# First entry: two low parts of w_spatial on GpSimd, a quarter of w_in later, value and gate by chunks

## The chip, the cores and the metric

The kernel runs on one core of one Trainium2 chip. The metric is the device time of one execution in microseconds (us). Five engines work side by side, each through a queue of its own in order: TensorE (PE, matmuls into PSUM; its weight loads are listed as PEld), VectorE (DVE), ScalarE (ACT), GpSimd (POOL) and SyncE (SP, which issues most DMAs).

## What is computed

For each of 8 batch entries (`b`), with 8 heads, 576 positions, head size 64, 32 packed queries, `d_model` 512 and `d_ff` 1024:

```python
p_packed = sm_attn(p, k, v)              # softmax attention of 32 packed queries
x = sm_attn(q, p_packed, p_packed)       # every position attends to the 32
h = relu(x @ w_in); u, v = h[..., :512], h[..., 512:]
v_n = (v - mean(v)) / sqrt(var(v) + 1e-6)        # over the 512
v_s = einsum('ts,bsd->btd', w_spatial, v_n) + b_spatial[None, :, None]
out = (u * v_s) @ w_out
```

`w_in` and `w_out` come in as 64-bit floats.

## The kernel before, in words

**Precision.** Matmuls of the feed-forward part use fp32r operands. A value is split in a high part (a cast to fp32r, `_h`) and a low part (the value less its high part, `_l`), and a product is made of the terms high-high, high-low and low-high.

**The value** (`FeedForward.value`, line 532) makes the right half of `h` in chunks of 128 positions: group `g` has the chunks 2g and 2g+1 (`js`), and group 2 is the tail of 64 positions with its two parts to be added. In entry 0 the three terms (`ns`) run one behind the other: a_h with m_h, a_h with m_l, a_l with m_h. Behind it come, chunk by chunk: `relu` (ACT, out of PSUM), `stats` (DVE, two operations), `inverse` (POOL, two operations on one column: add eps, power -1/2), `norm` (DVE), `norm_hi` (ACT cast into v_h) and `norm_lo` (v_l; on DVE, for some chunks of entry 0 on POOL). For the tail, `relu(2)` copies one part out on ACT and `relu_tail` adds it to the other, in PSUM, on DVE.

**The gate** (`FeedForward.gate`, line 647) multiplies the chunks of the normalised value by w_spatial. `es` are the four blocks of 128 of the 512 features, `cs` the chunks, and `parts` the terms: "h" and "m" take v_h with the high and the low part of w_spatial, "l" takes v_l with the high part, "t" is the tail and the bias. Each block has a PSUM quarter (`on(0)` to `on(3)`, tiles ps0 to ps3), and its result is copied out by `gate_keep` on ACT in entry 0.

**w_spatial** (line 184 on) lies in SBUF as four chunks and a tail (number 4). `spatial_hi(c)` casts its high part on ACT. The low part is made on PE in `spatial_rest(c)` (line 210): identity times the chunk, plus minus-identity times the high part, into PSUM; `spatial_lo(c)` (line 219) then copies it to `wsp_l` on ACT. `rest(lo, x, hi, eng)` (line 82) is a subtraction on a given engine.

**w_in** is loaded in four quarters, and each is turned from 64-bit to fp32 by `to_f32` (line 147), a generator with five steps, one for each `next`: an ACT conversion of the low word; two DVE operations on the high word (a shift with mask, and a combination); two POOL adds; an ACT `Abs`; and a last DVE operation that writes `w_in_sb`. `conv_u0` and `conv_u1` are the two quarters of the left half, which first serve `att.mix(0)` (line 1091). w_out is turned in the same way (`out01`, `out23`).

**Order.** PE, DVE, ACT and POOL execute in the order in which the program calls them (`InOrder`, line 35). Entry 0 is written out by hand (lines 892 to 1198), together with the first attention steps of the next entries; entries 1 to 7 run in a loop (line 1204) that the change doesn't touch. Behind the changed lines of entry 0 stand `nxt.pack_scores(by_turns(2, 3))` (line 1067), which writes ps2 and then ps3, and the rest of the gate for blocks 3 and 2.

Of the kernel before, what the change touches and what calls it, by code (L numbers as in the profile page):

```python
# [49 lines left out]
def body(ctx: ExitStack, tc, q, k, v, vt, p, w_in, w_sp, b_sp, w_out, out):  # L50
# [11 lines left out]
    pe, dve, act, pool = (  # L62
        InOrder(tc, e) if x in PIN else e
        for e, x in ((nc.tensor, "t"), (nc.vector, "v"), (nc.scalar, "s"), (nc.gpsimd, "g"))
    )
# [8 lines left out]
    def on(i):  # L74

        return lambda: psum.tile([P, 2, 512], F32, tag=f"ps{i}", name=f"ps{i}_t")
# [5 lines left out]
    def rest(lo, x, hi, eng=dve):  # L82
        eng.tensor_tensor(lo, x, hi.bitcast(F32), op=ALU.subtract)

    def mm(out_ap, lhsT, rhs, start, stop, more=False):

        pe.matmul(out_ap, lhsT=lhsT, rhs=rhs, start=start, stop=stop, skip_group_check=more)
# [31 lines left out]
    def load_v(b):  # L119
        v_sb = io.tile([P, NC + 1, H * D], F32, tag="v", name="v_sb")  # L120
        nc.sync.dma_start(v_sb[:, :NC, :], v[b])
        nc.sync.dma_start(v_sb[:, NC, : NJ * D], vt[b])
        loaded["v", b] = v_sb

    def load_q(b):
        qT = io.tile([P, 2, NJ, HS], F32, tag="qT", name="qT")
        for x in parts(b):
            nc.sync.dma_start(qT[:, x], q[b, :, x])
        loaded["q", b] = qT
# [17 lines left out]
    def to_f32(dst, raw, pool_, tag):  # L147

        low, high = raw[:, :, :, 0], raw[:, :, :, 1]
        act.activation(low, low.bitcast(U32), AF.Copy, scale=2.0**-29)
        yield
        bits = pool_.tile(raw.shape[:3], I32, tag=tag, name="bits")
        if dst is None:
            dst = bits.bitcast(F32)
        dve.tensor_scalar(
            bits, high, 3, 0x3FFFFFFF, op0=ALU.logical_shift_left, op1=ALU.bitwise_and  # L160
        )
        dve.scalar_tensor_tensor(
            bits, high, -0x40000000, bits, op0=ALU.bitwise_and, op1=ALU.bitwise_or
        )
        yield
        for j in range(raw.shape[1]):
            pool.tensor_tensor(bits[:, j], bits[:, j], low[:, j], op=ALU.add)
        yield
        size = high.bitcast(F32)
        act.activation(size, size, AF.Abs)  # L170
        yield
        dve.scalar_tensor_tensor(
            dst, size, LEAST, bits.bitcast(F32), op0=ALU.is_ge, op1=ALU.mult
        )
        yield dst
# [8 lines left out]
    wsp_h = const.tile([P, NC + 1, S], F32R, name="wsp_h")  # L184
    wsp_l = const.tile([P, NC + 1, S], F32R, name="wsp_l")
# [18 lines left out]
    def spatial(c):  # L204
        return st_sp[:, c, :] if c < NC else st_tail, slice(0, P if c < NC else TAIL)

    def spatial_hi(c):
        act.copy(wsp_h[:, c, :], spatial(c)[0])

    def spatial_rest(c, psum):  # L210

        x, _ = spatial(c)
        lo_ps[c] = ps = psum()
        for h in range(2):
            hs = slice(h * HS, (h + 1) * HS)
            mm(ps[:, h, :HS], ident, x[:, hs], True, False)
            mm(ps[:, h, :HS], minus, wsp_h[:, c, hs], False, True)

    def spatial_lo(c):
        rows = spatial(c)[1]  # L220
        act.copy(halves(wsp_l[rows, c, :]), lo_ps[c][rows, :, :HS])

    def split_bias():
        bias_h = two.tile([P, S], F32R, tag="o", name="bias_h")
        act.copy(bias_h[96:97, :], st_bias[96:97, :])
        act.copy(wsp_l[64:65, NC, :], st_bias[64:65, :])
        rest(wsp_l[96:97, NC, :], st_bias[96:97, :], bias_h[96:97, :])

    def load_out(e, n, pool_, tag):
        return load_f64(w_out[e * P : (e + n) * P, :], pool_, tag)  # L230
# [7 lines left out]
    def prepare_out(half, raw):  # L238

        for x in to_f32(None, raw, two, "vn"):  # L240
            yield
        sums["a1", half + 1] = x[:, :, :FH // 2]
        sums["a2", half + 1] = x[:, :, FH // 2 :]
# [59 lines left out]
    def halves(x):  # L303
        return x.rearrange("p (x t) -> p x t", x=2)
# [584 lines left out]
    def load_w_in(j, n, cols, pool_, tag):  # L889
        return load_f64(w_in[j * P : (j + n) * P, cols], pool_, tag)  # L890
# [16 lines left out]
    att, nxt, far, further = (Attention(b) for b in range(4))  # L907
# [35 lines left out]
    conv_u0 = to_f32(w_in_sb[:, 0:2, :FH], raw_u0, one, "p1")  # L943
# [10 lines left out]
    ff = FeedForward(0, att)  # L954
# [8 lines left out]
    spatial_hi(3)  # L963
    att.mix_hi(1)
    spatial_lo(0)
    att.query_norm(1, pool)
    att.query_tiles(); att.query_turn(0)
    raw_u1 = load_w_in(2, 2, lo_half, one, "wout_l")
    att.query_hi(0)
    att.mix_lo(1)  # L970
    att.query_turn(1)
    att.query_hi(1)
# [3 lines left out]
    ff.value(0, None, (0,), (1,))  # L976
    ff.value(0, None, (1,), (0,))
    ff.value(0, None, (1,), (1,))
    ff.value(0, None, (1,), (2,))
    ff.value(0, None, (0,), (2,))  # L980
    spatial_lo(1)
    next(conv_u0)
    next(conv_u0)
    att.query_lo(1, dve)
    raw01 = load_out(0, 2, one, "g_l")
# [1 line left out]
    ff.value(1, on(2), (0,), (0,))  # L987
    ff.value(1, None, (0,), (1,))
    ff.relu(0, (0,))
    spatial_hi(2)  # L990
    ff.value(1, None, (1,), (0,))
    ff.relu(0, (1,))
    ff.stats(0, (0,))
    ff.stats(0, (1,))
    next(conv_u0)
    spatial_lo(4)
    ff.inverse(0, (0,))
    ff.value(1, None, (1,), (1,))
    ff.value(1, None, (0,), (2,))
    ff.relu(1, (0,))  # L1000
    ff.stats(1, (0,))
    att.query_tail(1)
    ff.inverse(0, (1,))
    raw23 = load_out(2, 2, one, "g_h")
    load_v(1)
    next(conv_u0)
    spatial_rest(3, on(0))
    spatial_lo(3)
    ff.value(1, None, (1,), (2,))
    ff.relu(1, (1,))  # L1010
    ff.norm(0, (0,))
    ff.norm_hi(0, (0,))
    spatial_rest(2, on(3))
    ff.value(2, on(0))
    ff.norm(0, (1,))
    ff.gate((0,), "hm", (0,), on(2))
    ff.inverse(1, (0,))
    conv_u1 = to_f32(w_in_sb[:, 2:4, :FH], raw_u1, one, "p1T")
    ff.stats(1, (1,))
    spatial_lo(2)  # L1020
    load_q(1)
    ff.norm(1, (0,))
    ff.relu(2)
    ff.relu_tail()
    ff.stats(2)
    ff.gate((1,), "hm", (0,), on(3))
    ff.norm_hi(0, (1,))
    ff.gate((2,), "hm", (0, 1), on(1))
    ff.gate((1,), "hm", (1,))
    ff.gate((3,), "hm", (0, 1), on(0))  # L1030
    ff.inverse(1, (1,))
    ff.gate((0,), "hm", (1,))
    ff.norm_hi(1, (0,))
    ff.norm_lo(1, (0,), pool)
    ff.gate((1,), "hm", (2,))
    ff.gate((0,), "hm", (2,))
    next(conv_u1)
    ff.norm_lo(0, (0,), dve)
    ff.norm(1, (1,))
    ff.norm_hi(1, (1,))  # L1040
    ff.norm_lo(0, (1,), dve)
    ff.inverse(2)
    ff.norm(2)
    ff.norm_hi(2)
    ff.gate((0,), "hm", (3,))
    out23 = prepare_out(1, raw23)
    ff.gate((0,), "l", (0, 1))
    ff.gate((3,), "hm", (2, 3))
    ff.norm_lo(1, (1,), dve)
    ff.gate((0,), "l", (2, 3))  # L1050
    ff.norm_lo(2)
    ff.gate((1,), "hm", (3,))
    ff.gate((1,), "l", (0, 1))
    split_bias()
    ff.gate((1,), "l", (2, 3))
    ff.tail_hi(act.copy)
    ff.gate((0,), "t")
    next(out23)
    ff.gate((2,), "hm", (2, 3))
    next(conv_u1)  # L1060
    next(conv_u1)
    next(conv_u1)
# [141 lines left out]
    for b in range(1, B):  # L1204
        att, nxt, far = nxt, far, further
        further = Attention(b + 3) if b + 3 < B else None
        ff = FeedForward(b, att)
# [164 lines left out]
```

## Time and profile before

| | us |
|---|---|
| median of 3 runs | 395.8 |
| lowest, highest | 395.33, 396.11 |
| span of the profiled execution, first to last instruction | 393.6 |
| PE, DVE, ACT, POOL busy in the span | 384.0, 331.8, 204.6, 78.6 |

The profile gives one execution's span; the time of that execution around the span is not listed, and the runs' median is 2.2 us above it. A row of the timeline has the start and the duration in us, the engine, the line (L43 is the helper that records each operation), the operation, the tile written and the tiles read, the shapes and the count. In square brackets stands the idle time of the engine before it and what ended it. A row of a group has the count, the busy time in us and the mean in ns of one. A row of the chain has start, duration and what it was. Matmul ends are modelled, and spans on POOL are rough.

### The profile page before, as it was taken

The numbers are of one execution on the slowest core, as the hardware profiler recorded it, in microseconds if no ns is written. First come the engines' busy times: TensorE is split into PE (matmuls) and PEld (weight loads), VectorE is DVE, ScalarE is ACT, GpSimd is POOL, SyncE is SP. The second block draws the span as 40 slices with busy tenths as digits, with TensorE's granted clock in tenths as the row PEclk, the third lists the DMA queues.
The fourth block names the chain that finished last, engine by engine and source line by source line (L and its number), as shares of the span: only waits on it lengthen the run. The fifth ranks groups of instructions, "written<-read, shape, count | busy, mean of one in ns | idle before, by whom it ended". The sixth has DMA issues, their size and how long they took to land.

```text
span 393.6 us, 8856 instructions
## 1 busy us (share of the span) xinstructions
PE 384.0 (98%) x3758; PEld 354.7 (90%) x3758; DVE 331.8 (84%) x562; ACT 204.6 (52%) x306; POOL 78.6 (20%) x100
## 2 busy tenths in 40 slices
PE   5989999999999999999999999999999999999996
PEld 4768978899899899999899899998899889999995
DVE  2888799879999779998799869997699888988555
ACT  3579776656825365426734266344734264525221
POOL 3467426944000120002100030002100030004000
PEclk8799999999999999999999999999999999999999
DMA  7999148620720218011530206002300200021003
GB/s 301 407 372 416 39 146 351 248 92 32 288 81 31 92 47 323 3 57 65 225 139 32 90 8 235 2 30 92 116 8 25 97 2 0 2 85 38 2 0 120
DMA packets 17131, 46.61 MB, mean 118 GB/s; under 512 B 1346, under 2 KB 11586, under 8 KB 14276
## 3 DMA queue, kind: packets, MB, share of 16 engines
q1 hardware_dynamic: 16804, 45.84, 31.3%
q8 instruction: 29, 0.48, 0.5%
q10 hardware_dynamic: 288, 0.21, 0.2%
q14 instruction: 10, 0.08, 0.1%
HBM read 36.61 MB, written 9.44 MB: 117 GB/s over the span
## 4 chain that ended last, share of the span: by engine, by line
PE 94%; DMA 2%; ACT 2%; DVE 1%; POOL 0%; SPq 0%; issue 0%
PE ps_t L43 94%; DMA kT<-in_k 2%; ACT wsp_h L43 0%; ACT p1T L43 0%; POOL sm_t L43 0%; ACT sm_t L43 0%; ACT m_h L43 0%; DVE sm_t L43 0%; DVE mx L43 0%; ACT wsp_l L43 0%; DVE o L43 0%; SPq L116 0%; SPq L141 0%; ACT o L43 0%; DVE pp L43 0%
## 5 line engine op out<-in xcount | busy, mean ns | idle before, releaser
L43 PE MATMUL ps_t<-wsp_h,v_h 128*128 128x288 f32 x256 | 70.4, 298 | 0.0
L43 PE MATMUL ps_t<-wsp_l,v_h 128*128 128x288 f32 x256 | 69.6, 295 | 0.0
L43 POOL TENSOR_TENSOR rstd<-mv,eps 128x2 f32<-128x2 f32 (+2 forms) x26 | 7.3, 282 | 233.7 <-DVE mv L43 233.7
L43 PEld LDWEIGHTS ps_t<-wsp_h,v_h 128*128 128x128 f32 x256 | 48.0, 188 | 3.7 <-issue 1.9
L43 PE MATMUL ps_t<-t,wout_h 128*128 128x288 f32 x232 | 48.3, 294 | 0.0
L43 PEld LDWEIGHTS ps_t<-wsp_l,v_h 128*128 128x128 f32 x256 | 48.1, 188 | 0.0
L43 PE MATMUL ps_t<-wsp_h,v_l 128*128 128x288 f32 x256 | 43.9, 295 | 0.0
L43 PE MATMUL ps_t<-a_h,m_h 128*128 128x288 f32 x128 | 38.4, 300 | 0.0
L43 PEld LDWEIGHTS ps_t<-t,wout_h 128*128 128x128 f32 x232 | 38.0, 188 | 0.2 <-issue 0.2
L43 PEld LDWEIGHTS ps_t<-wsp_h,v_l 128*128 128x128 f32 x256 | 37.4, 188 | 0.5 <-issue 0.5
L43 PE MATMUL ps_t<-a_h,m_l 128*128 128x288 f32 x128 | 37.8, 295 | 0.0
L43 PE MATMUL ps_t<-a_l,m_h 128*128 128x288 f32 x128 | 37.7, 295 | 0.0
L43 ACT CAST g_h<-u 128x576 fp32r<-128x576 f32 x24 | 15.6, 673 | 33.2 <-DVE u L43 33.2
L43 PE MATMUL ps_t<-t,wout_l 128*128 128x288 f32 x116 | 32.3, 294 | 0.0
L43 PE MATMUL ps_t<-g_h,wout_l 128*128 128x288 f32 x104 | 29.0, 295 | 0.0
L43 PE MATMUL ps_t<-g_h,wout_h 128*128 128x288 f32 x104 | 29.0, 294 | 0.0
L43 DVE TENSOR_TENSOR u<-ps_t,u 128x576 f32<-128x576 f32 x28 | 21.0, 750 | 8.6 <-PE ps_t L43 8.5
L43 PE MATMUL ps_t<-m_h,a_h 128*128 128x512 f32 x80 | 25.9, 391 | 0.1
L43 PE MATMUL ps_t<-m_l,a_h 128*128 128x512 f32 x80 | 25.8, 389 | 0.0
L43 ACT CAST t<-g 128x576 fp32r<-128x576 f32 x21 | 14.2, 675 | 21.1 <-DVE g L43 20.4
L43 ACT ACTIVATE vr<-ps_t 128x1024 f32<-128x1024 f32 (+1 forms) x18 | 16.8, 932 | 15.2 <-PE ps_t L43 15.1
L43 PEld LDWEIGHTS ps_t<-a_h,m_h 128*128 128x128 f32 x128 | 24.1, 188 | 0.1
(142 smaller groups left out, 993.0 us busy)
## 6 DMA issues: line engine op xcount, KB each, us to landing
v_sb<-in_v SPq DMA_DIRECT2D x8, 1024.0 KB, 5.4
kT<-in_k SPq DMA_DIRECT2D x7, 1152.0 KB, 8.0
qT<-in_q SPq DMA_DIRECT2D x7, 1152.0 KB, 8.0
out_t<-o SPq DMA_DIRECT2D x17, 288.0 KB, 2.3
raw<-in_w_in SPq DMA_DIRECT2D x4, 1024.0 KB, 9.5
out_t<-prod SPq DMA_DIRECT2D x14, 288.0 KB, 2.4
raw<-in_w_out SPq DMA_DIRECT2D x2, 1024.0 KB, 12.9
kT<-in_k SPq DMA_DIRECT2D x2, 576.0 KB, 7.1
```

The lines of the kernel that those rows point to most:

```text
L43: return lambda *a, **k: self.tc.keep_in_program_order(call(*a, **k))
```

## The change

The low parts of w_spatial's chunks 3 and 2 are no longer made on PE and copied by ACT, but by one subtraction each on POOL (`spatial_lo_pool`). The quarter `conv_u0` takes its first step (ACT) earlier, and its third and fourth (POOL adds, ACT Abs) later, behind the low parts of the value. The terms of the value's group 1 come without the w_spatial products between them, and `value(2)` right behind them. The first block of the gate sits in ps3 and the second in ps2, where it was the other way round, and the gate's "h" and "m" terms go chunk by chunk over all four blocks, where block and chunk alternated. `query_tail(1)` stands ahead of the statistics.

```diff
+    def spatial_lo_pool(c):
+        rest(wsp_l[:, c, :], spatial(c)[0], wsp_h[:, c, :], pool)
...
     att.query_hi(0)
+    next(conv_u0)
     att.mix_lo(1)
...
+    ff.value(0, None, (0,), (2,))
     ff.value(0, None, (1,), (2,))
-    ff.value(0, None, (0,), (2,))
     spatial_lo(1)
-    next(conv_u0)
+    spatial_lo_pool(3)
     next(conv_u0)
     att.query_lo(1, dve)
...
     ff.relu(0, (0,))
+    ff.value(1, None, (1,), (0,))
+    ff.value(1, None, (1,), (1,))
+    ff.relu(0, (1,))
+    spatial_lo(4)
     spatial_hi(2)
-    ff.value(1, None, (1,), (0,))
-    ff.relu(0, (1,))
+    att.query_tail(1)
     ff.stats(0, (0,))
+    ff.inverse(0, (0,))
     ff.stats(0, (1,))
-    next(conv_u0)
-    spatial_lo(4)
-    ff.inverse(0, (0,))
-    ff.value(1, None, (1,), (1,))
+    ff.inverse(0, (1,))
     ff.value(1, None, (0,), (2,))
     ff.relu(1, (0,))
+    ff.value(1, None, (1,), (2,))
+    ff.norm(0, (0,))
+    ff.norm_hi(0, (0,))
+    ff.relu(1, (1,))
     ff.stats(1, (0,))
-    att.query_tail(1)
-    ff.inverse(0, (1,))
+    ff.inverse(1, (0,))
     raw23 = load_out(2, 2, one, "g_h")
     load_v(1)
-    next(conv_u0)
-    spatial_rest(3, on(0))
-    spatial_lo(3)
-    ff.value(1, None, (1,), (2,))
-    ff.relu(1, (1,))
-    ff.norm(0, (0,))
-    ff.norm_hi(0, (0,))
-    spatial_rest(2, on(3))
+    ff.norm(0, (1,))
+    ff.norm_hi(0, (1,))
+    spatial_lo_pool(2)
     ff.value(2, on(0))
-    ff.norm(0, (1,))
-    ff.gate((0,), "hm", (0,), on(2))
-    ff.inverse(1, (0,))
+    ff.gate((0,), "hm", (0,), on(3))
+    ff.gate((1,), "hm", (0,), on(2))
+    ff.gate((2,), "hm", (0,), on(1))
     conv_u1 = to_f32(w_in_sb[:, 2:4, :FH], raw_u1, one, "p1T")
     ff.stats(1, (1,))
-    spatial_lo(2)
     load_q(1)
     ff.norm(1, (0,))
     ff.relu(2)
+    ff.norm_hi(1, (0,))
     ff.relu_tail()
+    ff.gate((3,), "hm", (0,), on(0))
+    ff.inverse(1, (1,))
+    ff.gate((0, 1, 2, 3), "hm", (1,))
+    ff.norm(1, (1,))
+    ff.norm_hi(1, (1,))
     ff.stats(2)
...
+    ff.inverse(2)
+    ff.gate((0, 1, 2, 3), "hm", (2,))
     ff.norm_lo(1, (0,), pool)
...
     next(conv_u1)
     ff.norm_lo(0, (0,), dve)
-    ff.norm(1, (1,))
-    ff.norm_hi(1, (1,))
-    ff.norm_lo(0, (1,), dve)
-    ff.inverse(2)
     ff.norm(2)
     ff.norm_hi(2)
-    ff.gate((0,), "hm", (3,))
+    ff.norm_lo(0, (1,), dve)
+    next(conv_u0)
+    next(conv_u0)
+    ff.gate((0, 1, 2, 3), "hm", (3,))
     out23 = prepare_out(1, raw23)
-    ff.gate((0,), "l", (0, 1))
-    ff.gate((3,), "hm", (2, 3))
     ff.norm_lo(1, (1,), dve)
-    ff.gate((0,), "l", (2, 3))
     ff.norm_lo(2)
-    ff.gate((1,), "hm", (3,))
-    ff.gate((1,), "l", (0, 1))
+    ff.gate((0,), "l")
     split_bias()
-    ff.gate((1,), "l", (2, 3))
     ff.tail_hi(act.copy)
     ff.gate((0,), "t")
+    ff.gate((1,), "l")
     next(out23)
-    ff.gate((2,), "hm", (2, 3))
     next(conv_u1)
     next(conv_u1)
     next(conv_u1)
     ff.gate((1,), "t")
```

More of the change, by code (lines that the diff above doesn't have):

```diff
@@ L1023, in body @@
     ff.relu(2)
+    ff.norm_hi(1, (0,))
     ff.relu_tail()
-    ff.stats(2)
[L1026 to L1033, printed above, removed]
+    ff.gate((3,), "hm", (0,), on(0))
[3 more added lines that the diff above has]
+    ff.norm_hi(1, (1,))
+    ff.stats(2)
+    ff.inverse(2)
+    ff.gate((0, 1, 2, 3), "hm", (2,))
     ff.norm_lo(1, (0,), pool)
-    ff.gate((1,), "hm", (2,))
-    ff.gate((0,), "hm", (2,))
     next(conv_u1)
     ff.norm_lo(0, (0,), dve)
-    ff.norm(1, (1,))
-    ff.norm_hi(1, (1,))
-    ff.norm_lo(0, (1,), dve)
-    ff.inverse(2)
     ff.norm(2)
     ff.norm_hi(2)
-    ff.gate((0,), "hm", (3,))
+    ff.norm_lo(0, (1,), dve)
+    next(conv_u0)
+    next(conv_u0)
+    ff.gate((0, 1, 2, 3), "hm", (3,))
     out23 = prepare_out(1, raw23)
-    ff.gate((0,), "l", (0, 1))
-    ff.gate((3,), "hm", (2, 3))
     ff.norm_lo(1, (1,), dve)
-    ff.gate((0,), "l", (2, 3))
     ff.norm_lo(2)
-    ff.gate((1,), "hm", (3,))
-    ff.gate((1,), "l", (0, 1))
+    ff.gate((0,), "l")
     split_bias()
-    ff.gate((1,), "l", (2, 3))
     ff.tail_hi(act.copy)
     ff.gate((0,), "t")
+    ff.gate((1,), "l")
     next(out23)
-    ff.gate((2,), "hm", (2, 3))
     next(conv_u1)
```

## The prediction

> **What bounds the kernel now.** I read the page's busy shares first, then the chain that ended last in order of time, then PE's own waits.
>
> ```profile
> span 393.6 us, 8856 instructions
> PE 384.0 (98%) x3758; PEld 354.7 (90%) x3758; DVE 331.8 (84%) x562; ACT 204.6 (52%) x306; POOL 78.6 (20%) x100
> ...
> 27.31 30.59 PE ps_t L43 x316
> ...
> 58.23 331.71 PE ps_t L43 x3179
> ...
> PE ps_t L43 <- DVE pp L43: 0.2, 1, 0.2
> ```
>
> From 27.31 on the chain is TensorE, broken once, between 57.90 and 58.23, and the last line is that break: the only wait of PE's for another engine from 27.31 to 110. So a product that goes away there is worth its time, as long as no new wait opens, and every new PE wait before the block of `kT,pT` products at 48.21 moves the end by as much. What remains of the span behind that block is one uninterrupted PE queue, so I ask for one number: when does `nxt.pack_scores` start in the changed kernel, against 48.21?
>
> **What is removed.** Timeline of PE, the starts around the two calls of `spatial_rest` for chunks 3 and 2, one gate of one chunk, and one pair of value products:
>
> ```profile
> 31.94 0.61 PE L43 MATMUL ps_t<-m_h,a_l 128*128 128x512 f32 x2
> 32.40 0.65 PE L43 MATMUL ps_t<-st_sp,ident 128*128 128x288 f32 x2
> ...
> 33.63 0.63 PE L43 MATMUL ps_t<-m_h,a_l 128*128 128x512 f32 x2
> 34.09 0.65 PE L43 MATMUL ps_t<-st_sp,ident 128*128 128x288 f32 x2
> ...
> 35.33 0.62 PE L43 MATMUL ps_t<-m_h,a_h 128*128 128x512 f32 x2
> ...
> 36.25 0.29 PE L43 MATMUL ps_t<-wsp_h,v_h 128*128 128x288 f32 x1
> ...
> 36.77 0.29 PE L43 MATMUL ps_t<-wsp_h,v_h 128*128 128x288 f32 x1
> ...
> 48.21 1.97 PE L43 MATMUL ps_t<-kT,pT 64*32 64x288 f32 x32
> ```
>
> 33.63 - 32.40 and 35.33 - 34.09 give 1.23 + 1.24 = 2.47 us of PE gone. A value pair takes 32.40 - 31.94 = 0.46, one output block's gate of one chunk 36.77 - 36.25 = 0.53. The number of value and gate products is the same, only their order differs. ScalarE loses two copies into wsp_l; they lay beside PE and by themselves are worth nothing.
>
> **What is added: two subtractions on GpSimd, and whom they lock out.** `a_l<-at,a_h` on POOL has the shape of the new ones (576 columns, two SBUF inputs, fp32r out): 1.43 us. The rows of POOL and DVE side by side, each disturbed row beside an undisturbed one of its form:
>
> ```profile
> 27.10 1.43 POOL L43 TENSOR_TENSOR a_l<-at,a_h 128x576 fp32r<-128x576 f32 x1
> 28.03 1.06 DVE L43 TENSOR_SCALAR bits<-raw 128x1024 int32<-128x1024 int32 x1
> 43.70 0.69 DVE L43 TENSOR_SCALAR bits<-raw 128x1024 int32<-128x1024 int32 x1
> ...
> 73.61 1.44 POOL L43 TENSOR_TENSOR g_l<-u,g_h 128x576 fp32r<-128x576 f32 x1 [0.20 <-ACT g_h L43]
> 74.13 1.53 DVE L43 TENSOR_TENSOR sm_t<-sm_t,mx 128x576 f32<-128x576 f32 x1
> 78.33 0.69 DVE L43 TENSOR_TENSOR sm_t<-sm_t,sm 128x576 f32<-128x576 f32 x1
> ...
> 14.21 1.22 DVE L43 SCALAR_TENSOR_TENSOR w_in_sb<-raw,bits 128x1024 f32<-128x1024 f32 x1
> 14.52 3.33 POOL L43 TENSOR_TENSOR bits<-bits,raw 128x512 int32<-128x512 int32 x2 [3.51 <-ACT raw L43]
> 15.35 1.28 DVE L43 TENSOR_SCALAR rtot<-tot 128x2 f32<-128x2 f32 x1
> 8.47 2.54 POOL L43 TENSOR_TENSOR bits<-bits,raw 128x512 int32<-128x512 int32 x2 [5.94 <-DVE bits L43]
> ```
>
> DVE's 0.69 at 28.03 became 1.06: it got through about when POOL's 1.43 ended (28.53, less 0.1). The 0.69 at 74.13 became 1.53: POOL's began at 73.61 and ended at 75.05. In the other direction, POOL's pair of adds (2.54 alone) took 3.33 because DVE's 14.21 ran to 15.43, and then DVE's two-column operation at 15.35 took 1.28, behind the first add. So DVE operations with two SBUF inputs, and its tensor-scalar operations, exclude a POOL operation and are excluded by it for its whole length; who waits longest goes next. Reductions, statistics and operations that read PSUM aren't touched.
>
> One thing these rows leave open: the combined operation (1.22 at 14.21) is seen holding POOL up, never held up itself. The Trainium skill ("SBUF — State Buffer", section "Who interferes with whom") lets a DVE operation with two SBUF inputs contend with a POOL operation that reads SBUF in either order, the second to issue "fully blocks". By that rule the sum below is +5.4; if the combined operation is never held, +4.2.
>
> This matters since DVE has hardly any room here and its order is written out. The walk below takes each engine's queue in the new program order; an operation starts when its engine is free, its inputs are there and the other engine's hold is over. Durations are from the rows above and these groups (between 24 or 26 and 50; POOL between 18 and 60):
>
> ```profile
> L43 DVE BATCH_NORM_STATS2 bn<-vr 128x6 f32<-128x512 f32 x4 | 2.8, 694 | 0.4 <-ACT vr L43 0.3
> L43 DVE SCALAR_TENSOR_TENSOR bits<-raw,bits 128x1024 int32<-128x1024 int32 x2 | 2.5, 1226 | 0.1
> L43 DVE TENSOR_SCALAR vr<-vr,mv,rstd 128x512 f32<-128x512 f32 x4 | 2.1, 536 | 0.5 <-POOL rstd L43 0.5
> L43 DVE TENSOR_TENSOR vr_tail<-ps_t,part 64x512 f32<-64x512 f32 x1 | 0.7, 683 | 0.0
> ...
> L43 ACT CAST v_h<-vr 128x512 fp32r<-128x512 f32 x4 | 2.4, 618 | 1.4 <-DVE vr L43 1.4
> ...
> L43 POOL TENSOR_TENSOR rstd<-rstd,neg_half 128x1 f32<-128x1 f32 x4 | 2.7, 686 | 0.3
> L43 POOL TENSOR_TENSOR v_l<-vr,v_h 128x512 fp32r<-128x512 f32 x1 | 1.3, 1298 | 0.4 <-ACT v_h L43 0.4
> ```
>
> Walked the same way, the kernel before gives 48.03 for the 48.21 of the trace, with 0.08 of PE wait.
>
> *Chunk 3's subtraction.* It asks at 28.5, waits for DVE's bits operation and runs 29.0 to 30.45. DVE's next, the combined one of 1.23 us, can't start at 29.13 but at 30.35; behind it on DVE stand `query_lo(1)` (to 32.24), `query_tail`, and only then the statistics of value chunk 0. PE's third term of chunk 2 is late: **wait 0.35**. Statistics 32.39 to 33.30, inverse on POOL to 34.18 (its two steps about 0.8), norm to 34.85, cast on ACT to 35.50, first gate at 35.59. Without the removed products PE has its values done at 34.11: **wait 1.48**. Moving the adds of the w_in quarter away from here does free POOL for this inverse, but DVE arrives late.
>
> *Chunk 2's subtraction.* In POOL's queue it stands right behind the inverse of value chunk 2, and the norm that needs this inverse can only ask once it is there: POOL is already holding (36.84 to 38.27) when the norm asks at 36.90. It ends at 38.72 and holds up what stands behind it on DVE, the sum of the tail's parts (to 39.31). That sum reads ps0, which the gate of block 3 now wants fourth, where it wanted it only after seven chunks before. PE has done three gates by 37.19 and starts the fourth at 39.36: **wait 2.17**.
>
> *The w_in quarter.* Its adds (2.54 alone) come behind the low part of value chunk 2 on POOL, and that behind the tail's inverse. The norm of the tail is passed by POOL in the same way (POOL 42.47 to 43.76; norm ends at 44.21), then DVE's low parts of chunks 1 and 3 alternate with the two adds and end at 45.97 and 47.73. PE goes through 13 gates and half of block 0's low part from 39.36 to 46.82, and meets the other half at 47.81: **wait 0.99**. The tail's low part (48.35) and the bias's (49.13) follow on DVE, block 0's last products at 49.18: **wait 0.84**. Its Abs on ScalarE stands ahead of the bias copies, and is covered there. Where its first step (1.17 on ScalarE) now stands, ScalarE had an idle stretch, and its data are there, landed 13.1 after an issue at 11.89:
>
> ```profile
> 28.14 0.67 ACT L43 CAST a_h<-at 128x576 fp32r<-128x576 f32 x1 [1.11 <-DVE at L43]
> 11.89 0.39 SPq L141 DMA_DIRECT2D raw<-in_w_in  x1
> raw<-in_w_in SPq DMA_DIRECT2D x1, 1024.0 KB, 13.1
> ```
>
> That step costs nothing then; if `at` came sooner, up to 1.1 us at the second half of a_h. The loads that SP issues among the moved calls (w_out, v, q of the next entry) fill buffers whose last readers lie before 27 us and aren't moved, so SP's queue stays as it is.
>
> *The exchange of ps2 and ps3.* Rows of ScalarE before:
>
> ```profile
> 45.69 1.19 ACT L43 ACTIVATE raw<-raw 128x1024 f32<-128x1024 f32 x1 [0.40 <-DVE bits L43]
> 46.91 0.64 ACT L43 COPY u<-ps_t 128x576 f32<-128x576 f32 x1
> 48.32 0.64 ACT L43 COPY u<-ps_t 128x576 f32<-128x576 f32 x1 [0.77 <-PE ps_t L43]
> ```
>
> `pack_scores` begins in ps2. That was block 0's, copied out at 46.91, well ahead; now it is block 1's, copied out last. Ahead of both copies on ScalarE stands the Abs of the other w_in quarter, which waits for DVE's bits (now to 51.09): Abs (1.19) to 52.29, copies to 53.35, `pack_scores` at 53.41. PE was done at 51.31: **wait 2.10**. With a punctual DVE this would still cost 0.7 (one copy).
>
> **The sum.** 0.35 + 1.48 + 2.17 + 0.99 + 0.84 + 2.10 = 7.93 of waits, less 2.47 removed and 0.08 that was there: +5.4 us. Bounds of what the rows don't settle: no row shows a DVE operation that asks within 0.1 us of POOL's start. If POOL takes hold only 0.15 after its recorded start, DVE passes it at the tail's norm and the walk gives +4.4, at 0.3 +3.5. If the combined operation alone isn't held up (no row shows it waiting) it is +4.2, if the holds end 0.3 early +3.2; held to the recorded ends +6.1. I take +4.9, midway between the walk as recorded and the one at 0.15. The profile gives a span of 393.6 and no time around it; the median of the runs is 395.8, 2.2 above it, which I carry over: 395.8 + 4.9 = **400.7 us**, own range 398.8 to 402.
>
> **The rivals.**
>
> *PE also loses its clock.* Busy times by stretches of 2 us (PE second, the granted clock third from the end):
>
> ```profile
> 6.00:8.00 2.00, 0.00 (x0) 0.02 (x1) 1.69 (x2) 1.15 (x1) 0.00 (x0) 0.96 1.01 408
> 8.00:10.00 2.00, 1.83 (x32) 0.47 (x32) 0.23 (x1) 1.15 (x1) 1.53 (x2) 0.50 1.04 427
> ...
> 14.00:16.00 2.00, 1.63 (x23) 1.44 (x25) 2.00 (x3) 1.87 (x4) 1.49 (x1) 0.83 1.02 409
> ```
>
> After some 2.5 us of idleness PE ran at 0.50 until about 14.7. A wait of 2.17 is close to that. If the clock halves for 6 us behind it, the PE work there takes 6 x 0.5 = 3 us longer, and the waits after it (0.99 + 0.84 + 2.10 = 3.9) hide most of that; behind the 2.10 at `pack_scores` nothing hides it. So 0 to 4.3 more, I say 2.8 (the 3 at `pack_scores`, less what the next DVE wait gives back): 403.5. For it: two waits above 2 us. Against it: both are shorter than that idleness. The Trainium skill ("TensorE: Matmul & The Clock Gate", Part 1) has the drop after an idle window of about 3.4 us; by that alone this case would not come, though this trace shows it after 2.5.
>
> *The hold costs a part.* The low parts and the norms get in between, only the two subtractions delay DVE, by one hold each where it stands on PE's path: about 1.2 + 1.2 less the 0.4 that the walk without holds gains: +2.0, 397.8 (396.6 to 398.8). For it: every tie that I decided for POOL lies within 0.4 us. Against it: the queue orders put POOL first at both subtractions.
>
> *No hold matters.* The same walk without any hold: PE waits 0.12 for the first gate, 1.10 for block 3 and 0.92 at ps2, 2.14 less 2.47 and 0.08: -0.4, **395.4**; up to 396.0 if the inverses take some 0.3 longer each, as those that POOL shared with a DVE norm did (group mean 0.69). Then the change does what it says, and the queue orders give the gain back. Against it: the disturbed rows above.
>
> *Not slower: the gain stays.* POOL gets rid of the early adds, so the inverses come 1.3 us sooner, and the exclusion falls on POOL each time, because DVE is always ahead of it. Then the 2.47 counts, less the one copy of 0.7 at ps2: 394.0 (393.3 to 394.9). It decides if DVE's combined bits operation starts by 29.2 and the norm of chunk 2 takes under 0.7. Against it: POOL has been waiting since 28.5 when that operation can ask at all.
>
> **Chances.** Forecast 0.58; clock 0.08; part 0.12; no hold 0.09; gain stays 0.13. A difference within 0.2% (0.8 us) is what a measurement can't tell from none. Slower 0.78, same 0.08, faster 0.14 (the no-hold case gives 0.01 to it). For 8 in 10 the range reaches down to the no-hold case and leaves out the kept gain and the upper part of the clock's: 395.4 to 402.6.
>
> **What would show it.** DVE's combined bits operation near 29 to 31.6 lasts over 2 us in the trace; the norm near 37 lasts about 1.8; PE waits for v_h at the first gate (1.5), for vr_tail at block 3 (2.2) and for `u` at `kT,pT` (2.1); the `kT,pT` block starts near 53 rather than 48.21; behind it the order and lengths on PE are as before. If those DVE operations keep 1.23 and 0.54, the forecast is wrong at its root; if they are long and PE doesn't wait, my queue order is.

## The result, and the profile after

The changed kernel takes 401.45 us (median; 401.0 to 401.93) beside 395.8 (395.33 to 397.57) for the kernel before: a ratio of 1.0134, 95% interval 1.0119 to 1.0150 (it isn't the quotient of the two medians, which is 1.0143). That is +5.65 us where +4.9 was forecast, slower as predicted and inside the range.

The page of the changed kernel (span, busy time) and the last piece of its chain of waits:

```profile
span 400.1 us, 8831 instructions
PE 384.1 (96%) x3746; PEld 354.2 (89%) x3746; DVE 336.9 (84%) x562; ACT 203.9 (51%) x304; POOL 81.0 (20%) x102
...
64.33 332.15 PE ps_t L43 x3182
```

PE is as busy as before (384.1 beside 384.0) although products went away: some of the rest ran slower (below). The last uninterrupted PE piece is 332.15 us long, beside 331.71 before (over all kernels run here it varies from 331.67 to 332.18), so what is lost lies ahead of it. It starts at 64.33 where it was 58.23. Of these 6.10, 0.61 lie before the changed stretch: the first value product is at 27.92, beside 27.31, behind a wait of PE of 1.2 us for a load of w_spatial; over all kernels run here that start varies from 27.3 to 28.2. The one trace of the kernel before has no such wait, 11 of the 12 variants below have it (0.5 to 1.6), so whether the change has a part in these 0.61 isn't shown. So kernels are compared below by the **stretch** from the first `m_h,a_h` product to the start of that last piece: 30.92 us before (58.23 - 27.31), 36.41 after (64.33 - 27.92), **+5.49**.

PE's waits in the changed kernel, 20 to 400 us (tile waited for: us in all, times, longest):

```profile
PE ps_t L43 <- DVE vr_tail L43: 1.6, 1, 1.6
PE ps_t L43 <- ACT v_tail L43: 1.4, 1, 1.4
PE ps_t L43 <- DMA st_sp<-in_w_sp: 1.2, 1, 1.2
...
PE ps_t L43 <- ACT u L43: 0.7, 1, 0.7
PE ps_t L43 <- ACT vr L43: 0.7, 1, 0.7
PE ps_t L43 <- DVE p1T L43: 0.5, 1, 0.5
PE ps_t L43 <- DVE v_l L43: 0.3, 1, 0.3
PE ps_t L43 <- ACT v_h L43: 0.2, 1, 0.2
```

Where the list of before has one wait of 0.2 behind 27.31, there are now waits at seven places: six ahead of the `kT,pT` block, and `p1T` behind it. Their idle times understate the loss, since PE's first product after a wait also takes longer to the next start (0.23 instead of 0.13); I therefore read the starts of the products. Timeline of PE after:

```profile
27.92 0.70 PE L43 MATMUL ps_t<-m_h,a_h 128*128 128x512 f32 x2
...
34.22 0.73 PE L43 MATMUL ps_t<-m_h,a_l 128*128 128x512 f32 x2 [0.69 <-ACT vr L43]
...
36.09 0.40 PE L43 MATMUL ps_t<-wsp_h,v_h 128*128 128x288 f32 x1 [0.21 <-ACT v_h L43]
...
46.60 0.29 PE L43 MATMUL ps_t<-wsp_h,v_l 128*128 128x288 f32 x1
...
48.57 0.35 PE L43 MATMUL ps_t<-wsp_h,v_tail 128*128 128x288 f32 x1
...
50.83 2.02 PE L43 MATMUL ps_t<-wsp_h,v_l 128*128 128x288 f32 x8
52.65 0.44 PE L43 MATMUL ps_t<-wsp_h,v_tail 128*128 128x288 f32 x1
...
54.54 1.24 PE L43 MATMUL ps_t<-kT,pT 64*32 64x288 f32 x32 [0.73 <-ACT u L43]
```

| stretch of PE | before | after | growth | forecast |
|---|---|---|---|---|
| first value product to first gate product | 36.25 - 27.31 = 8.94, 6.47 without the removed 2.47 | 36.09 - 27.92 = 8.17 | 1.70 | 0.35 + 1.48 = 1.83 |
| first gate product to the `kT,pT` block | 48.21 - 36.25 = 11.96 | 54.54 - 36.09 = 18.45 | 6.49 | 2.17 + 0.99 + 0.84 + 2.10 = 6.10 |

1.70 + 6.49 - 2.47 = +5.72 at `kT,pT`, beside +5.4 of the walk. Behind it three differences take this to +5.49, but for 0.02. The `kT,pT` block takes 1.17 to the next product where it took 1.90 before (there its second half starts only at 49.01, behind ScalarE's copy of `u` that ends at 48.96), which is 0.73 less. PE waits for `p1T`, 0.63 by the starts. The old break at 57.90 is 0.11 shorter. Now the cause, in the timeline of DVE, and then of POOL:

```profile
28.64 1.07 DVE L43 TENSOR_SCALAR bits<-raw 128x1024 int32<-128x1024 int32 x1
29.75 2.33 DVE L43 SCALAR_TENSOR_TENSOR bits<-raw,bits 128x1024 int32<-128x1024 int32 x1
...
37.39 1.52 DVE L43 TENSOR_SCALAR vr<-vr,mv,rstd 128x512 f32<-128x512 f32 x1
...
42.51 4.03 DVE L43 TENSOR_SCALAR vr_tail<-vr_tail,mv,rstd 64x512 f32<-64x512 f32 x1 [0.71 <-POOL rstd L43]
46.47 1.28 DVE L43 TENSOR_TENSOR v_l<-vr,v_h 128x512 fp32r<-128x512 f32 x2
```

```profile
29.12 1.87 POOL L43 TENSOR_TENSOR wsp_l<-st_sp,wsp_h 128x576 fp32r<-128x576 f32 x1
...
37.22 1.41 POOL L43 TENSOR_TENSOR wsp_l<-st_sp,wsp_h 128x576 fp32r<-128x576 f32 x1
...
42.45 1.29 POOL L43 TENSOR_TENSOR v_l<-vr,v_h 128x512 fp32r<-128x512 f32 x1
43.70 2.56 POOL L43 TENSOR_TENSOR bits<-bits,raw 128x512 int32<-128x512 int32 x2
```

Three DVE operations are long, each beside a POOL operation: the combined bits operation takes 2.33 instead of 1.23, the norm of chunk 2 takes 1.52 instead of 0.54, the norm of the tail takes 4.03 instead of about 0.5 and ends (46.54) 0.28 after POOL's second add (46.26). The DVE operations behind them have their usual lengths.

### The profile page after: what moved, and what is told of

The parts are those of the page before. It is cut to its first block, busy times and chain, and to the rows that moved or that the text cites. A ratio compares the mean times of both kernels' runs of the same rounds, so it can differ in the third digit from the quotient of the medians.

```text
span 400.1 us, 8831 instructions
## 1 busy us (share of the span) xinstructions
PE 384.1 (96%) x3746; PEld 354.2 (89%) x3746; DVE 336.9 (84%) x562; ACT 203.9 (51%) x304; POOL 81.0 (20%) x102
## 4 chain that ended last, share of the span: by engine, by line
PE 84%; DVE 7%; DMA 5%; ACT 2%; issue 1%; POOL 0%; POOLq 0%
PE ps_t L43 84%; DMA st_sp<-in_w_sp 4%; DVE bits L43 2%; DMA raw<-in_w_in 1%; DVE vr_tail L43 1%; DVE vr L43 1%; DVE bn L43 1%; ACT wsp_h L43 0%; POOL rstd L43 0%; DVE nmax L43 0%; DVE at L43 0%; ACT v_tail L43 0%; DVE w_in_sb L43 0%; DVE sm L43 0%; DVE m_l L43 0%
## 5 line engine op out<-in xcount | busy, mean ns | idle before, releaser
L43 PE MATMUL ps_t<-wsp_h,v_l 128*128 128x288 f32 x256 | 45.1, 300 | 0.4 <-DVE v_l L43 0.3
```

What stands on the lines that cost most here:

```text
L43: return lambda *a, **k: self.tc.keep_in_program_order(call(*a, **k))
```

## The experiments

The **theory** is that POOL's long operations hold DVE's, and that the late DVE results make PE wait. The **rival** is that the new written order by itself (products gone that covered latencies, terms chunk by chunk) makes PE wait, whatever POOL does. A **third** candidate is the exchange of ps2 and ps3 at `pack_scores`. All measured numbers first; times are medians, ratios are against the kernel before with 95% intervals, the stretch is that of the profiled execution, less the 30.92 of before:

| kernel | stretch from, to | growth | time, us | ratio |
|---|---|---|---|---|
| after | 27.92, 64.33 | +5.49 | 401.45 | 1.0134 (1.0119 to 1.0150) |
| no_subs | 27.44, 61.95 | +3.59 | 399.76 | 1.0099 (1.0079 to 1.0120) |
| no_adds | 28.18, 61.69 | +2.59 | 398.73 | 1.0067 (1.0050 to 1.0085) |
| no_pool | 27.61, 58.78 | +0.25 | 396.47 | 1.0010 (1.0000 to 1.0020) |
| subs_pe | 27.73, 63.90 | +5.25 | 401.2 | 1.0133 (1.0114 to 1.0151) |
| b_subs_pool | 27.84, 60.12 | +1.36 | 397.45 | 1.0038 (1.0025 to 1.0051) |
| subs_dve | 27.85, 63.66 | +4.89 | 400.41 | 1.0109 (1.0095 to 1.0122) |
| memset | 28.06, 63.16 | +4.18 | 400.5 | 1.0113 (1.0095 to 1.0130) |
| lo2_dve | 27.84, 63.22 | +4.46 | 400.68 | 1.0114 (1.0100 to 1.0127) |
| swap | 28.09, 63.59 | +4.58 | 401.18 | 1.0126 (1.0111 to 1.0141) |
| adds_last | 27.75, 62.95 | +4.28 | 401.61 | 1.0136 (1.0109 to 1.0163) |
| reorder1 | 28.08, 60.73 | +1.73 | 398.0 | 1.0043 (1.0029 to 1.0056) |
| reorder2 | 27.60, 57.75 | -0.77 | 395.37 | 0.9983 (0.9974 to 0.9993) |

The kernel before had a median of 396.1 to 396.2 beside each of these experiments. In three of the profiled executions (after, no_subs, subs_dve) PE's clock fell ahead of the `kT,pT` block, and ScalarE's second copy of `u` waited 0.26, 0.38 and 0.50 for the slower products; in the other variants with the changed order the two copies run back to back. About that much of the three growths belongs to the fall of the clock.

**no_subs: the changed kernel without the two subtractions** (the low parts of w_spatial's chunks 2 and 3 are left out; they are zero from the start).

```diff
+    pool.memset(wsp_l[:, 2:4, :].bitcast(F32), 0.0)
...
-    spatial_lo_pool(3)
...
-    spatial_lo_pool(2)
```

> The changed kernel without the two subtractions on POOL: the low parts of w_spatial's chunks 2 and 3 are left out (set to zero once, at the start), everything else is as changed. Theory A (POOL's operations hold up DVE): the combined bits operation is back to 1.23 us, the norm of value chunk 2 to about 0.55, PE's wait for block 3 falls from 1.6 to under 1; what the low part of value chunk 2 and the w_in adds hold up on DVE stays (the tail's norm stays near 4 us). Walk: +3.0 over the kernel before, 398.8. Theory B (the new order itself costs, not POOL): as the changed kernel, +5.6, 401.4.

Measured: +3.59. The subtractions are worth 5.49 - 3.59 = 1.90 of the loss. DVE's rows:

```profile
29.26 1.23 DVE L43 SCALAR_TENSOR_TENSOR bits<-raw,bits 128x1024 int32<-128x1024 int32 x1
...
35.80 0.52 DVE L43 TENSOR_SCALAR vr<-vr,mv,rstd 128x512 f32<-128x512 f32 x1
...
40.02 4.03 DVE L43 TENSOR_SCALAR vr_tail<-vr_tail,mv,rstd 64x512 f32<-64x512 f32 x1 [0.71 <-POOL rstd L43]
```

Exactly the two operations beside the subtractions are short again, the third is not. The result is nearer to +3.0 than to +5.6; it is 0.6 above. The walk had no fall of the clock, and in this execution the clock fell to 0.50 between 48 and 50, which gives 0.38 of it. PE's wait for block 3 is 0.5, under 1 as expected.

**no_adds: without the two POOL adds of `conv_u0`** (so the values of that w_in quarter lack their low words).

```diff
-        for j in range(raw.shape[1]):
+        for j in range(raw.shape[1] if adds else 0):
...
-    conv_u0 = to_f32(w_in_sb[:, 0:2, :FH], raw_u0, one, "p1")
+    conv_u0 = to_f32(w_in_sb[:, 0:2, :FH], raw_u0, one, "p1", adds=False)
```

> The changed kernel without the two POOL adds of the late w_in quarter (its values are wrong then), all else as changed. Theory A: the tail's norm is held only by the low part of value chunk 2, about 1.5 us instead of 4.0; walk +3.7 over before, 399.5. If the adds didn't count: +5.3, 401.2.

Measured: +2.59, more gain than the walk had (+3.7). The adds are worth 2.90. Timeline of DVE:

```profile
42.77 1.51 DVE L43 TENSOR_SCALAR vr_tail<-vr_tail,mv,rstd 64x512 f32<-64x512 f32 x1 [0.71 <-POOL rstd L43]
```

The tail's norm now stands behind one POOL operation (the low part, 1.3) instead of three, and takes 1.51 instead of 4.03.

**no_pool: neither subtractions nor adds, and the low part of value chunk 2 on DVE** (low parts and low words left out as in the two kernels above, by the same edits). The edit beside those:

```diff
-    ff.norm_lo(1, (0,), pool)
+    ff.norm_lo(1, (0,), dve)
```

> The changed kernel with all three of POOL's long visits to DVE's stretch taken away: the two subtractions left out (low parts set to zero at the start), the two adds of the late w_in quarter left out (its values are wrong), and the low part of value chunk 2 made by DVE. Order, PSUM exchange and everything else as changed. Theory A (POOL holds up DVE): the 2.47 us of PE come nearly all back against the waits that the order has (block 3 for the tail's sum, the copies out of ps2 and ps3): +0.6 over before, 396.4; no DVE norm over 0.6 us. Theory B (order): +3 or more, 398.8.

Measured: +0.25 in the stretch, +0.3 in the time. This decides against the rival: with the order of the changed kernel as it is and only POOL's long operations gone, the loss is 0.25 of 5.49. DVE's rows, and what PE still waits for:

```profile
29.43 1.22 DVE L43 SCALAR_TENSOR_TENSOR bits<-raw,bits 128x1024 int32<-128x1024 int32 x1
...
40.80 0.54 DVE L43 TENSOR_SCALAR vr_tail<-vr_tail,mv,rstd 64x512 f32<-64x512 f32 x1 [0.71 <-POOL rstd L43]
```

```profile
PE ps_t L43 <- ACT u L43: 1.3, 1, 1.3
...
PE ps_t L43 <- ACT vr L43: 0.7, 1, 0.7
...
PE ps_t L43 <- DVE vr_tail L43: 0.5, 1, 0.5
```

1.3 + 0.7 + 0.5 = 2.5, and another 0.5 for `p1T` behind the `kT,pT` block: the order's own waits eat the 2.47 that the removed products gave. So the change would bring nothing even if POOL held nobody.

**subs_pe: the changed order, with the low parts of chunks 3 and 2 made on PE as before.**

```diff
-    spatial_lo_pool(3)
+    spatial_rest(3, on(0))
+    spatial_lo(3)
...
-    spatial_lo_pool(2)
+    spatial_rest(2, on(1))
+    spatial_lo(2)
```

> The changed kernel with the two low parts made on PE and copied by ACT again, as before the change; w_in and all orders as changed. Theory A: 2.47 us of PE work come back, and the two holds go; by the walk nearly even, +5.0 over before, 400.8, since the holds by the low part of value chunk 2 and the w_in adds remain. Theory B: the PE work comes on top of the order's loss, +8, 403.9.

Measured: +5.25, beside +5.0 of the theory. Putting 2.47 us of products back costs no time against the changed kernel: at these places the subtractions take on DVE what they give on PE. DVE's combined operation is 1.23 and the norm of chunk 2 0.52 in it; the tail's norm is still 4.04, and PE waits 1.4 for `v_tail`.

**b_subs_pool: the kernel before, with only the two subtractions put on POOL,** behind `spatial_lo(1)` and behind the first inverse of group 1.

```diff
     spatial_lo(1)
+    spatial_lo_pool(3)
...
-    spatial_rest(3, on(0))
-    spatial_lo(3)
...
-    spatial_rest(2, on(3))
...
     ff.inverse(1, (0,))
+    spatial_lo_pool(2)
...
-    spatial_lo(2)
```

> The kernel before with one part of the change alone: the low parts of chunks 3 and 2 by subtraction on POOL (behind spatial_lo(1) and behind the inverse of value chunk 2), PE's products and ACT's copies for them gone; w_in, value, gate and PSUM as before. Theory A: PE's 2.47 us are given back and more by DVE, late first at the bits operation (over 2 us instead of 1.23) and at a norm: walk +2.0, 397.8. Theory B (the subtractions are harmless): -2.0 to -2.5, 393.5.

Measured: +1.36, on the side of the theory (+2.0) and against a kept gain (-2.0 or less). In the old order too the subtractions take 2.47 from PE and lose more than that (2.47 + 1.36 = 3.83). Timeline of DVE:

```profile
29.65 2.34 DVE L43 SCALAR_TENSOR_TENSOR bits<-raw,bits 128x1024 int32<-128x1024 int32 x1
...
38.19 1.35 DVE L43 TENSOR_SCALAR vr<-vr,mv,rstd 128x512 f32<-128x512 f32 x1
```

**subs_dve: the two subtractions on DVE, at the same places.**

```diff
+    def spatial_lo_dve(c):
+        rest(wsp_l[:, c, :], spatial(c)[0], wsp_h[:, c, :], dve)
...
-    spatial_lo_pool(3)
+    spatial_lo_dve(3)
...
-    spatial_lo_pool(2)
+    spatial_lo_dve(2)
```

> The changed kernel with the two subtractions on DVE, at the same places of the order. Theory A: DVE has 1.4 us more of its own work but isn't locked out by them; its combined bits operation is back to 1.23, the norm of value chunk 2 to 0.55; what the late POOL operations hold up stays. Walk: +4.4, 400.5. If only the amount of DVE's work counted and no hold: +6.5, 402.5 (the changed kernel plus 1.4, less the removed 0.4).

Measured: 400.41 in the time, beside 400.5 of the walk, and +4.89 in the stretch, beside +4.4; 0.50 of that goes with the fall of the clock. In this trace the two take DVE 1.13 (beside a_l on POOL) and 0.75; from POOL they made DVE's operations 1.10 and 0.98 longer (2.33 - 1.23, 1.52 - 0.54) and the gain of the whole is 0.6 in the stretch, 1.0 in the time. So doing it on the busy engine is no dearer than being locked out by the idle one; the rest of the loss stays with the adds.

**memset: two fills on POOL in place of each subtraction** (low parts of chunks 2 and 3 left out). A fill writes, and reads nothing.

```diff
-        rest(wsp_l[:, c, :], spatial(c)[0], wsp_h[:, c, :], pool)
+        pool.memset(wsp_l[:, c, :].bitcast(F32), 0.0)
+        pool.memset(wsp_l[:, c, :].bitcast(F32), 0.0)
```

> The changed kernel with each subtraction on POOL replaced by two fills of the same place with zero (the low parts are left out): POOL is busy at the same places but reads nothing from SBUF. Theory A with a hold only for POOL operations that read: DVE's combined bits operation is back at 1.23 us, and the time is that without the subtractions, about 399.6. Theory A with a hold for any POOL operation: the bits operation or the norm is long again, by as much as a fill lasts. Theory E (POOL's own queue, its inverses late, costs): as the changed kernel, 401.4.

Measured: 400.5, between the two numbers, so the time decides nothing. The rows do. DVE and POOL side by side:

```profile
28.78 1.58 DVE L43 TENSOR_SCALAR bits<-raw 128x1024 int32<-128x1024 int32 x1
29.25 1.64 POOL L43 MEMSET wsp_l<- 128x576 f32 x2
30.40 1.22 DVE L43 SCALAR_TENSOR_TENSOR bits<-raw,bits 128x1024 int32<-128x1024 int32 x1
...
36.75 1.38 POOL L43 MEMSET wsp_l<- 128x576 f32 x2
36.94 0.67 DVE L43 TENSOR_SCALAR vr<-vr,mv,rstd 128x512 f32<-128x512 f32 x1
```

The combined operation starts at 30.40 and takes its 1.22 though the fills go on to 30.89: a writer doesn't hold it, where a subtraction made it 2.33. The Trainium skill ("SBUF — State Buffer", section "Who interferes with whom") states just this: two SBUF inputs on DVE contend with a POOL instruction that reads SBUF, not with one that only writes. For the writer this trace agrees (1.22), for the reader the changed kernel's (2.33). The tensor-scalar operations are another kind: beside fills the first was 1.58 where it was 1.07 in the changed kernel, and the norm 0.67 instead of 0.54, so they are lengthened, though the norm not by a whole fill. POOL's own queue has a part here too: the inverse of chunk 3 stands behind the fills, and its norm waits 0.45 for it, which it doesn't in no_subs. How much of the time that makes isn't separated.

**lo2_dve: the low part of value chunk 2 on DVE,** so that the tail's norm meets two POOL operations (the adds) and not three.

```diff
-    ff.norm_lo(1, (0,), pool)
+    ff.norm_lo(1, (0,), dve)
```

> The changed kernel with the low part of value chunk 2 made by DVE, so that behind the tail's inverse POOL goes straight to the two adds of the late w_in quarter. Theory A1 (a DVE operation that waits gets in between two POOL operations): the tail's norm takes 1.5 to 1.8 us, behind one add. Theory A2 (POOL keeps its hold over a row of adds): about 2.8 us, behind both. Time by the walk: +4.7 over before with A1, 400.8; a little later with A2, 401.3.

Measured: 400.68, +4.46 in the stretch, sooner than the walk had for either case (400.8 and 401.3), so the time doesn't choose between them. The rows of POOL and DVE do:

```profile
42.97 2.56 POOL L43 TENSOR_TENSOR bits<-bits,raw 128x512 int32<-128x512 int32 x2
43.04 2.78 DVE L43 TENSOR_SCALAR vr_tail<-vr_tail,mv,rstd 64x512 f32<-64x512 f32 x1 [0.72 <-POOL rstd L43]
```

The norm waits for both adds: 2.78, not 1.5 to 1.8. Together with 4.03 behind three and 1.51 behind one this shows that here POOL kept the hold from one operation to its next while DVE waited. The turn-taking that I had read out of the kernel before doesn't hold at this place.

**swap: `pack_scores` in the order ps3, ps2,** which takes away the exchange of the banks at this one place.

```diff
-    nxt.pack_scores(by_turns(2, 3))
+    nxt.pack_scores(by_turns(3, 2))
```

> The changed kernel with pack_scores writing ps3 first and then ps2, so that it begins in the quarter of block 0, as before the change. Theory A: the copies out of both quarters are late for DVE's sake, so only one copy is saved: +4.9 over before, 400.7. Theory C (the exchange of ps2 and ps3 is the main loss): 2.1 less, +3.5, 399.3.

Measured: +4.58 in the stretch, nearer to +4.9 than to +3.5; the time differs from the changed kernel's by 0.3, which its interval doesn't separate. PE waits 1.0 for `u` in place of 0.7. The exchange is no main cause: behind late DVE results both banks' copies come late.

**adds_last: the adds of `conv_u0` moved behind those of `conv_u1`,** and with them its Abs and its last DVE operation to later places.

```diff
-    next(conv_u0)
-    next(conv_u0)
     ff.gate((0, 1, 2, 3), "hm", (3,))
...
     next(conv_u1)
+    next(conv_u0)
     ff.gate((1,), "t")
...
     next(conv_u1)
+    next(conv_u0)
     next(out01)
```

> The changed kernel with the two POOL adds and the Abs of the late w_in quarter moved behind the other quarter's adds (and its last DVE operation behind pack_max). Theory A: the tail's norm is held only by the low part of value chunk 2, 1.1 us instead of 3.5; `pack_scores` about 2.3 sooner than in the changed kernel; behind it DVE has one operation more before p1T, which takes 1.1 of it back: +4.2 over before, 400.0. Theory B: no gain, +5.6 to +6.7, 401.4 to 402.5.

Measured: the profiled execution has +4.28 (its own time is 400.28, the lowest), but the median is 401.61, no better than the changed kernel and within what the expectation gave the rival (401.4 to 402.5): as an improvement this failed. The tail's norm is short again in the trace (1.51), as the theory had it. The trace shows where a gain was given back. The `kT,pT` block starts 50.97 - 27.75 = 23.22 after the first value product (26.62 in the changed kernel), 3.40 sooner; at the end of the stretch 1.21 are left. Of PE's waits:

```profile
PE ps_t L43 <- ACT p L43: 2.2, 1, 2.2
```

`conv_u0`'s scratch is the buffer tag "p1", which `pack_exp` of the next entry takes for its result. It can't be written until the quarter's last DVE operation has read it, and that now stands behind two late adds: in the trace `p`, at 56.39, waits for DVE's write of `w_in_sb`. A moved step also moves the release of its buffer. What made the other executions longer than the profiled one isn't shown.

**reorder1 and reorder2: new orders for the whole stretch,** worked out with the walk of the prediction and the holds as measured by then. PE's 2.47 stay removed, and so do the low parts on PE. In reorder1 the subtraction for chunk 3 is on POOL, the other on DVE, the second half of a_l on POOL, the adds behind the gate's start. The core of it, in the new order (most lines around it are moved too):

```diff
-    att.query_lo(1, dve)
+    att.query_lo(1, pool)
...
     ff.norm(0, (0,))
+    spatial_lo_pool(3)
     ff.inverse(0, (1,))
...
     ff.norm(1, (0,))
+    spatial_lo_dve(2)
     ff.norm_hi(1, (0,))
```

> A version of the changed kernel ordered by the walk, so that POOL's long operations fall beside DVE operations that aren't locked: chunk 3's low part on POOL behind the first norm, chunk 2's on DVE, both w_in quarters, value and gate reordered, pack_scores from ps3. All is computed. Theory A with the walk's numbers: TensorE ends this stretch 1.05 sooner than in the kernel before, 395.1 against 396.1. If holds matter that the walk doesn't have: no better than before, 396 to 398.

Measured: +1.73, a miss by 2.8, though 3.8 better than the changed kernel in the stretch. The combined bits operation took 2.34 again, beside the second half of a_l on POOL; PE waited 1.3 for `m_l`, 0.9 for `v_h` and 0.7 for `vr`. In reorder2 both subtractions are on DVE, the bits operation comes before the second half of a_l, the tail's value products stand between the two halves of group 1's last term, and the adds run beside the statistics of the tail:

```diff
     ff.norm(0, (0,))
+    ff.value(2, on(0))
     ff.relu(1, (0,))
     ff.norm_hi(0, (0,))
     ff.value(1, None, (1,), (2,))
...
     ff.stats(1, (0,))
+    spatial_lo_dve(3)
     ff.stats(1, (1,))
...
     ff.norm(1, (0,))
+    spatial_lo_dve(2)
...
     ff.gate((2,), "hm", (1,))
+    next(conv_u0)
     ff.relu(2)
...
-    nxt.pack_scores(by_turns(2, 3))
+    nxt.pack_scores(by_turns(3, 2))
```

> Another order found in the same way, with other places for the two subtractions and the adds. Walk: 1.0 sooner than the kernel before, 395.1; if holds matter that the walk doesn't have, 396 to 398.

Measured: -0.77 in the stretch, 395.37 (394.78 to 396.48) beside 396.12: it lies 0.17% (0.07 to 0.26%) under the kernel before, and 6 us under the changed kernel. Against the kernel before that is less than the 0.8 us which the prediction called the limit of a measurement, and the interval leaves out 1 only narrowly. PE's waits from 20 on, and rows of DVE and POOL:

```profile
PE ps_t L43 <- ACT v_h L43: 0.8, 1, 0.8
...
PE ps_t L43 <- DVE pp L43: 0.7, 1, 0.7
```

```profile
34.41 0.72 DVE L43 TENSOR_TENSOR wsp_l<-st_sp,wsp_h 128x576 fp32r<-128x576 f32 x1
...
36.76 0.75 DVE L43 TENSOR_TENSOR wsp_l<-st_sp,wsp_h 128x576 fp32r<-128x576 f32 x1
...
42.70 0.53 DVE L43 TENSOR_SCALAR vr_tail<-vr_tail,mv,rstd 64x512 f32<-64x512 f32 x1
```

```profile
37.89 2.79 POOL L43 TENSOR_TENSOR bits<-bits,raw 128x512 int32<-128x512 int32 x2
```

No DVE operation on PE's path is held for more than about 0.1: the adds (2.79) run while DVE waits for the tail's part and reads PSUM, and the tail's norm takes 0.53. The wait for `vr` is gone too. What PE still loses is 0.8 at the first gate and a break of 0.7 for `pp` later.

## Why the prediction was right, and where not

**The core held: POOL's long operations lock DVE out, and PE pays.** Both signs named for it came: the combined operation at 29.75 lasted 2.33 (over 2 forecast), the norm at 37.39 lasted 1.52 (1.8 forecast). The `kT,pT` block came at 54.54, or 53.93 without the later start of 0.61, where the walk had 53.41. no_pool shows that POOL's long operations make 5.49 - 0.25 = 5.24 of the loss.

**The combined operation is held.** That was taken from the Trainium skill's rule alone ("SBUF — State Buffer", section "Who interferes with whom"), with +4.2 as the price if it were not so. 2.33 beside a subtraction, and 1.23 without (no_subs) or 1.22 beside fills (memset), settle it for the rule.

**The removed 2.47** came as computed, and the order's own waits took them back (no_pool: 2.5). The walk without holds had -0.4 here; measured was +0.25, so the "no hold" rival's account of the order was 0.65 too good.

**Value, forecast 0.35 + 1.48, measured 1.70 in all, but at another place.** The first-gate wait was 0.21, not 1.48, because PE had already waited 0.69 for `vr` at 34.22, between the two halves of group 1's last term. That wait is missing from the prediction; the 0.35 at the third term of chunk 2 came as 0.22 (32.12 to 32.80, less 0.46). `relu(1, (0,))` stands between these halves in the order, so the second half waits until ScalarE has read the first out of the same PSUM tile; in the kernel before, w_spatial's products stood there and covered it. That tile as the reason is read from the order and the named releaser; reorder2, with other products at that place, has no such wait.

**Block 3, forecast 2.17: idle 1.60,** 1.77 by starts (37.66 to 39.56, less 0.13). The mechanism was as told: norm of chunk 2 passed by the subtraction, tail's sum late. The size was off by 0.4, of which 0.3 are the norm, 1.52 and not 1.8.

**The tail and the low parts, forecast 0.99 + 0.84 = 1.83: idle 0.30 + 1.40, by the starts 0.88 + 1.73** (46.60 to 48.57 less 1.09, and 48.57 to 50.83 less 0.53, which is what eight and four such products take in the kernel before). Two steps failed. The first is "DVE's low parts of chunks 1 and 3 alternate with the two adds". Nothing alternated: the tail's norm stood behind all three POOL operations at once (4.03), and the low parts then ran freely (1.28 for two). DVE made up for it, and was done with the tail's low part at 48.47, 0.49 sooner than walked (48.35 + 0.61). The second is "Its Abs on ScalarE stands ahead of the bias copies, and is covered there". Rows of ScalarE after:

```profile
46.58 0.62 ACT L43 CAST v_tail<-vr_tail 64x512 fp32r<-64x512 f32 x1 [4.40 <-DVE vr_tail L43]
47.10 1.14 ACT L43 ACTIVATE raw<-raw 128x1024 f32<-128x1024 f32 x1
...
49.65 0.62 ACT L43 CAST v_tail<-v_tail 64x512 fp32r<-64x512 f32 x1
```

The late norm holds up the cast, and behind the cast stand the Abs, two bias copies and the tail's second copy, for which PE waits (to 50.27). DVE's last operand for these products, the bias, was ready at 49.72, where the walk had it (49.13 + 0.61). So the wait for the low parts came about as forecast, and the tail's was twice as long, since ScalarE's queue behind the late norm ended later than DVE's.

**ps2 at `pack_scores`, forecast 2.10: idle 0.73, by the starts 2.09** (50.83 to 54.54, less 1.09 + 0.53). The rest went into PE's clock. Stretches of 2 us of the changed kernel (PE busy first after the length, granted clock third from the end):

```profile
50.00:52.00 2.00, 1.68 (x9) 1.68 (x10) 1.97 (x3) 1.60 (x3) 0.06 (x1) 0.73 0.04 8
52.00:54.00 2.00, 1.81 (x8) 1.46 (x7) 0.84 (x1) 1.72 (x3) 2.00 (x2) 0.50 0.00 0
```

The eight products at 50.83 took 52.65 - 50.83 = 1.82 instead of about 1.09 (44.91 to 46.00 before), the four tail products 0.24 each instead of 0.13: 1.2 more, nearly all of it inside a time in which PE would have waited for `u` anyway (0.26 isn't, for which ScalarE's second copy of `u`, at 53.85, waits for PE). So the clock rival came, but neither at its place nor at its price: behind the waits of 0.30 and 1.40, with 1.2 of slower work, mostly hidden, where 2.8 more were said. The price was wrong because it put the halved clock behind the wait for `u`; there it was back at 0.91 and 1.00.

**The number.** The walk as recorded had +5.4; +4.9 was chosen, midway to a POOL that takes hold 0.15 late. Measured are +5.49 in the stretch and +5.65 in the time: that correction was for nothing. POOL passed the norms that asked 0.06 (tail) and 0.17 (chunk 2) after its recorded start. That the sum came so close is in part luck: block 3 was 0.4 dearer in the forecast than in the trace, the tail 0.9 cheaper, and behind `kT,pT`, where the walk had PE as before, the shorter block (0.73) and the wait for `p1T` (0.63) nearly cancel.

## What to carry to other kernels

An operation put on an idle GpSimd isn't free while VectorE is busy with tensor-scalar or two-input operations: count its length as time that can be taken from VectorE (here 1.4 us of subtraction cost VectorE 1.0 to 1.1), and ask which engine waits for VectorE next; here the same subtractions done on VectorE itself cost less. Products that are removed from TensorE may have been the cover of a latency (a read of a PSUM tile by ScalarE), so walk the in-order queues to the next consumer before counting them as gain. If a step is moved later, its scratch buffer comes free later too; look up who takes that buffer next.

## What the runs showed of the hardware that was not expected

**Who gets in next isn't settled by who waits longest.** Behind POOL operations in a row the tail's norm took 1.51 (one), 2.78 (two) and 4.03 (three). The other way round, in reorder1, a norm and four low parts on DVE made a one-column POOL operation wait:

```profile
42.60 2.81 POOL L43 TENSOR_TENSOR rstd<-mv,eps 64x1 f32<-64x1 f32 x1 [1.29 <-DVE mv L43]
```

```profile
42.87 2.48 DVE L43 TENSOR_TENSOR v_l<-vr,v_h 128x512 fp32r<-128x512 f32 x4
```

At 28.64 in the changed kernel, though, DVE's bits operation got in between two POOL operations (1.07; the subtraction behind it then took 1.87 instead of 1.41). What decides between the two outcomes stays open.

**The clock fell after short idleness.** In the changed kernel PE was idle 0.30 and 1.40 within 4 us, and the clock went to 0.73 and 0.50; in no_subs and subs_dve, behind waits of 0.2 or 0.3 and 1.4, it fell to 0.50 too (48 to 50, and 50 to 52). In subs_pe and swap the same waits (0.3 and 1.4) left it at 1.00. The Trainium skill ("TensorE: Matmul & The Clock Gate", Part 1) gives an idle window of about 3.4 us for the drop; the changed kernel's trace doesn't agree with that figure. What tells the executions apart isn't shown here.
